# A long convolution and an MLP on one core: every transpose moved to TensorE, the cosine made from an absolute value, inverse rest columns evicted pair by pair, and a new order

## The chip, the cores and the metric

The kernel runs on one core of a Trainium2 chip. The metric is the device time of one execution in microseconds. Engines are named as in the profile: PE (TensorE), ACT (ScalarE), DVE (VectorE), POOL (GpSimd), SP (SyncE, which here only issues DMAs).

## The reference

Sequence length S = 2048, width D = 640, F = 1728, batch 1, bfloat16. Two branches share a layer norm:

```python
x = A_q
xn = _layernorm(x, axis=-1)
# branch A
k_shift = sum over t of k_pad[:, t:t + S, :] * shift_k[:, ks - 1 - t]     # ks = 4
kv = k_shift * v
y = irfft(rfft(kv padded to 2S) * rfft(ssm_k padded to 2S))[:S] + kv * ssm_D
s = xn * y
# branch B
g = silu(gelu(xn @ w1 + b1) @ w2 + b2)
return x + s * g
```

Branch A is a convolution along the sequence with a filter of length 2048 for each of the 640 columns; branch B is a two-layer MLP. (The sum is written short here; in the reference it is a loop over four shifts.)

## The kernel before

**Layout.** Rows lie as [128 partitions, 16 tiles, 640 columns]. A tile i holds one row for each partition; `x`, `xn`, `K` (the filter), `k` and `v` all have this form. The DMA work is large: 31.30 MB are read from DRAM and 18.35 MB written, the inputs and three scratch buffers of 128 x 32 rows, each written and read once. The buffer `kvl` holds k and v, and later what is loaded back from scratch.

**Branch A** is a Fourier transform in two stages, by matmuls. A table `W` [128, 16, 128] holds sines and cosines of the first stage: DVE makes the angles as whole numbers modulo 8192 (`wq`), ACT's Sin turns them into W (`ws`), in two groups (tiles 0 to 3 and 4 to 15). Stage one (`stage1`) multiplies each of the 16 tiles of K, and of the product kv, by its slice of W (`K1_i`, `U1_i` for the first 512 columns, `K1r_g`, `U1r_g` for the other 128 columns of four tiles together). The results are evicted from PSUM to the buffer `st` (`Ke`, `Ker`, `Ue`, `Uer`; st has room for four stores) and stored to `scrK` and `scrU` (`Ks_r`, `Us_r`, eight each, 640 KB). Since partitions change their meaning between the stages, the data go through DRAM: `KL_s` and `UL_s` read them back in another order. The loads can start only when all eight stores have landed.

Stage two takes 8 groups s. A small table F2 makes 32-point transforms of K and U (`K2`, `U2`, `X2` for the rest columns of both), evicted by `Kf` and `Uf`; DVE multiplies the two (`pr` for 512 columns, `qr` for the rest); the table I1 transforms back (`i1_s`, and `i1r` for the rest columns of two groups together), evicted by `ie` and `ier`; `cs_s` stores to `scrC`, `cl_r` reads back after all eight. Last come `i2_i` with the inverse table `G`, which is W with each 128x128 slice transposed, `ym_i` (DVE, times xn), `ad_i` (DVE, plus x) and the output store `os_i`.

The kv product itself is DVE work: five groups `kv0` to `kv4`, each four products with the shift weights and three sums, then times v (L524, L528, L531, L533). The weights are broadcast by `wm` and `we`.

**Branch B.** `bn`, `ep`, `rs`, `xn` are the layer norm (`ep`, `rs` on POOL mostly). The MLP's first layer needs xn transposed, `xnT`, in four chunks of four tiles. In the kernel before, tiles 0 to 7 (chunks 0 and 1) are transposed on PE (`xt`, L422, five 128x128 transposes a tile, copied out of PSUM by `xe`); chunks 2 and 3 are transposed by one DMA each (`xT2`, `xT3`, L429), and G by a third one (`gt`, L496), all from SP. `f1_c_ft_r` is the first layer (L450, `f1h` L464 for the half tile), `ge` the Gelu on ACT, `f2_i_n` the second layer for half a tile's columns (L486), `si` the Silu on ACT, `gx` the product with xn on DVE. For tiles 12 to 15 f2 comes after the convolution's end.

**Order.** Every operation is an entry of a plan, and the string `ORDER` lists all of them in the order in which they are issued. A suffix names the engine where there is a choice (`/D` DVE, `/A` ACT, `/P` POOL, `/S` SP; `/C` makes PE use two column halves), and the numbers after a colon are slots: PSUM banks (eight), quarters of st, or buffers for the loads. Each engine works through its own entries strictly in this order, so an entry that waits holds up what stands behind it on its engine. All evictions are issued in `evict` (L179 in the profile), told apart there by the tile they write: `st` is stage one, `kvl` stage two and inverse, `xnT` the transposes. `WARM` gives the number of warm-up matmuls (L699) that are put between the first entries, on zeros.

Of the kernel before, what the change touches and what calls it, by code (L numbers as in the profile page):

```python
# [112 lines left out]
def h3_block(ctx: ExitStack, tc: tile.TileContext, x_d, k_d, v_d, sk_d, K_d, D_d, w1_d, b1_d, w2_d, out_d):  # L113
# [123 lines left out]
    for g in range(2):  # L237
        a, b = TB[g], TB[g + 1]

        def wq(e, a=a, b=b):  # L240
# [4 lines left out]
            nc.vector.tensor_single_scalar(out=Pc[:, a:b, :], in_=Pc[:, a:b, :], scalar=L - 1, op=ALU.bitwise_and)
            nc.vector.tensor_single_scalar(out=Pm[:, a:b, :], in_=Pm[:, a:b, :], scalar=L - 1, op=ALU.bitwise_and)

        def ws(e, a=a, b=b):
            wv = W_t[:, a:b, :].rearrange("p t (k c) -> p t k c", c=2)
            for c, p_ in enumerate((Pc, Pm)):  # L250
                nc.scalar.activation(out=wv[:, :, :, c], in_=p_[:, a:b, :], func=ACT.Sin, scale=sc, bias=cst[:, 0:1])
# [293 lines left out]
    for s in range(NG):  # L545
# [81 lines left out]
        if z == 1:  # L627
# [12 lines left out]
            for y in range(2):  # L640

                def ier(e, y=y, pb=pb, Us=R["U"][y]):
                    q = sorted(b.slot for b in pb)
                    src = ps_t[:].rearrange("p (m n) c -> p m n c", n=2)[:, q[0] // 2:q[1] // 2 + 1:(q[1] - q[0]) // 2, :, 128 * y:128 * y + 128]
                    evict(e, Us.v[:, :, CA:D].rearrange("p (m n) c -> p m n c", n=2), src)
# [2 lines left out]
                R["C"][y].append(cw)
                op("ier_%d" % (s - 1 + y), "ACT|DVE", ier, reads=pb + R["p"][2 * y:2 * y + 2], writes=[cw], hold=[R["U"][y]])
# [57 lines left out]
ORDER = """
zz c0 grid fix xl0 id b1l skl warm9:0 warm1:1 xl3 Kl1 warm3:0 wq1 bn0 bn4 bn5 warm0:1 Kl3 warm8:0 mh bn6 Dl sm0 xl1 wm3:2 wm0:0
ep0/P warm2:4 ws1 K1_4:6.0 we0 xl2 bn7 one1 sm1 we3 K1_7:4.1 wm1:0 ep3/P rs3 Ke_7 we1 bn1 rs0 Ke_4 warm5:2 warm4:3 w1l1
K1r_3:4.2.3 xn5 Ker_6 warm6:2 K1_12:0 wm2:2 bn3 warm7:6 kl0 xn4 w1l0 xn7 w1l3 Ker_7 xn0 K1r_1:6 K1_14:4 xn6 ep1/P we2 Ke_12 w1l2  # L710
xt4:2.0 one0 xe4/D xt7:3 rs1 K1_5:0 Ke_14 Ke_5 xn1 xt6:2 xt5:4 Ker_2 xe7/D xe6/D w1l4 b1c xe5/D xt1:5.1 Ker_3 K1_6:0 K1_13:2 Ke_6
wq0 f1_1_0_0:4.1 xt0:6 xe1/D bn2 Ke_13 Kl0 K1_15:0 xe0 f1_1_9_0:5 f1_0_9_0:7.0 vl3 sm2 sm3 f1_0_2_0:6 f1_1_2_0:2 ep2/P kv0_1m:0
f1_1_8_0:3 rs2 ws0 ss Ke_15 xn3 ge_1_8_0 Ks_3/P kv0_0:1 xn2 Ks_2 xt3:0 kl1 vl0 f1_1_3_0:1 f1_1_5_0:3 xe3 kv0_1a xt2:0 ge_0_2_0
ge_1_2_0 Da ge_1_3_0 f1_1_4_0:2 ge_1_9_0 ge_1_5_0 kv0_2m:0 ge_1_4_0 f1_0_0_0:1 sx f1_0_3_0:5 xe2/D f1_0_11_0:6 f1_0_4_1:0 kv0_2a
Ks_6/P ge_0_3_0 ge_1_0_0 ge_0_11_0 ge_0_9_0 f1_0_8_1/C:3 f1_0_5_2:2 K1_0:4.2 ge_0_0_0 K1r_0:6.0 ge_0_8_1 ge_0_5_2 f1_0_4_0/C:1
f1_0_10_0/C:3 Ke_0 f1h_1:2 f1_0_1_1/C:4 kv0_3m:0 ge_0_10_0 Ker_1 ge_0_1_1 kv0_3a Ker_0/D geh_1 f1_1_10_0/C:3 f1_1_12_0/C:5 kv0_4
# [78 lines left out]
```

## Time and profile before

| | |
|---|---|
| times of three runs | 194.02, 194.5, 195.72 us; median 194.5 |
| span of the profiled execution | 191.4 us |
| its own time | not given apart from the span; the median of the runs is 3.1 us over it |
| PE busy | 175.2 us, 92% |
| DVE busy | 156.2 us, 82% |
| ACT busy | 145.4 us, 76% |
| POOL busy | 27.0 us, 14% |
| DMA | 51.82 MB, mean 271 GB/s |
| chain that ended last | PE 52%, DMA 22%, DVE 11%, ACT 8% |

Three engines are full at the same time. A busy share is an average over stages, though: up to about 40 us the DMA engines are full with inputs (over 400 GB/s for most of 10 to 35 us), then stage one and the MLP run beside one another, from about 88 us stage two, from about 164 us the last inverse step and the output. What an idle stretch of an engine costs is read from what ended it: the waits name the engine and line that waited, and who released it.

### The profile page before, as it was taken

Reading aid. Unit: us, or ns where it says so; the run is one execution under the profiler, and the core shown is the slowest. Engines: PE = TensorE matmul, PEld = TensorE weight load, DVE = VectorE, ACT = ScalarE, POOL = GpSimd, SP = SyncE. Lnnn points to the kernel's source line nnn. Section 1 sums busy time; section 2 is a strip of 40 time slices with the busy share of each in tenths; the row PEclk is TensorE's granted clock in tenths of the full one; section 3 lists DMA queues with packets and bytes.
Section 4 is the critical chain, followed back from the end, with each engine's and each line's share of the span. In section 5 each row is a group of like instructions: output and inputs, shape, how many; then the busy total and the mean of one; then the engine's idle time right before and its main releaser. Section 6 shows DMA issues by size and latency. Waiting matters only on the chain.

```text
span 191.4 us, 5365 instructions
## 1 busy us (share of the span) xinstructions
PE 175.2 (92%) x2262; PEld 104.8 (55%) x2262; DVE 156.2 (82%) x261; ACT 145.4 (76%) x227; POOL 27.0 (14%) x58
## 2 busy tenths in 40 slices
PE   7799996899999978996969999999999999989990
PEld 2235564685676545564535444444555569668780
DVE  7989797699998999799996876967999630669992
ACT  4789994999999949965866997979889867832110
POOL 4196820000100000123200100030000113000000
PEclk9969999999999999999999999999999999999998
DMA  6999999954999986769996179599712376991384
GB/s 189 375 421 419 409 423 422 424 205 155 351 358 395 335 312 276 310 241 315 364 233 191 30 252 205 170 384 339 120 39 102 140 274 206 420 415 62 102 290 160
DMA packets 26683, 51.82 MB, mean 271 GB/s; under 512 B 9122, under 2 KB 19747, under 8 KB 26276
## 3 DMA queue, kind: packets, MB, share of 16 engines
q1 hardware_dynamic: 23200, 40.06, 60.5%
q0 software_dynamic: 2304, 10.49, 14.4%
q10 hardware_dynamic: 1156, 0.95, 1.5%
q8 instruction: 17, 0.28, 0.6%
q14 instruction: 6, 0.05, 0.1%
HBM read 31.30 MB, written 18.35 MB: 259 GB/s over the span
## 4 chain that ended last, share of the span: by engine, by line
PE 52%; DMA 22%; DVE 11%; ACT 8%; POOL 2%; issue 1%; SPq 1%; ACTq 0%; DVEq 0%
PE ps L450 21%; PE ps L486 15%; DMA kvl<-scrU 7%; DMA kvl<-scrC 5%; DMA scrK<-st 4%; ACT st L179 4%; PE ps L603 4%; PE ps L358 3%; DMA x<-in_ssm_k 3%; PE ps L560 2%; DMA scrU<-st 2%; DVE xn L672 2%; DVE x L676 2%; PE ps L699 2%; ACT kvl L179 2%
## 5 line engine op out<-in xcount | busy, mean ns | idle before, releaser
L486 PE MATMUL ps<-w,hT 128*64 128x320 bf16 (+4 forms) x644 | 65.8, 294 | 0.0
L450 PE MATMUL ps<-xnT,w 128*64 128x512 bf16 (+5 forms) x550 | 62.3, 324 | 2.8 <-ACT st L179 2.4
L486 PEld LDWEIGHTS <-hT 128*64 128x64 bf16 (+3 forms) x644 | 45.6, 105 | 19.2 <-issue 6.4
L179 ACT CAST kvl<-ps 128x1024 bf16<-128x1024 f32 (+2 forms) x52 | 42.1, 847 | 10.7 <-PE ps L574 4.5
L450 PEld LDWEIGHTS <-w 128*64 128x64 bf16 (+1 forms) x550 | 33.9, 106 | 25.6 <-issue 9.2
L179 ACT CAST st<-ps 128x1024 bf16<-128x1024 f32 (+1 forms) x44 | 37.4, 958 | 6.1 <-DMA scrK<-st 2.5
L454 ACT ACTIVATE hT<-ps,b1f 128x512 bf16<-128x512 f32 (+2 forms) x71 | 36.8, 619 | 3.7 <-PE ps L450 3.3
L179 DVE CAST kvl<-ps 128x1024 bf16<-128x1024 f32 (+1 forms) x24 | 25.9, 1089 | 11.0 <-ACT kvl L179 5.2
L490 ACT ACTIVATE sl<-ps 128x320 bf16<-128x320 f32 (+1 forms) x33 | 14.1, 447 | 14.6 <-PE ps L486 8.2
L593 DVE TENSOR_TENSOR st<-kvl 128x2048 bf16<-128x2048 bf16 x16 | 19.2, 1219 | 0.4 <-ACT kvl L179 0.4
L528 DVE TENSOR_TENSOR kvl<-kvl 128x2560 bf16<-128x2560 bf16 (+1 forms) x15 | 18.3, 1221 | 0.8 <-DMA kvl<-in_k 0.6
L531 DVE TENSOR_TENSOR kvl<-kvl 128x2560 bf16<-128x2560 bf16 (+1 forms) x15 | 18.3, 1223 | 0.4
L492 DVE TENSOR_TENSOR xn<-xn,sl 128x320 bf16<-128x320 bf16 (+1 forms) x33 | 9.9, 310 | 9.9 <-ACT sl L490 9.9
L672 DVE TENSOR_TENSOR xn<-ps,xn 128x640 bf16<-128x640 f32 x16 | 12.7, 820 | 2.1 <-PE ps L668 2.0
L392 DVE BATCH_NORM_STATS2 stats<-x 128x6 f32<-128x320 bf16 x32 | 13.8, 474 | 0.1
L560 PE MATMUL ps<-kvl,F 64*32 64x512 bf16 x256 | 10.4, 380 | 1.4 <-ACT st L179 1.4
L699 PE MATMUL ps<-hT 128*128 128x512 bf16 x20 | 8.5, 577 | 1.2 <-DVE hT L223 1.2
L490 ACT ACT_TABLE_LOAD x5 | 6.4, 1283 | 3.6 <-PE ps L486 3.6
L603 PE MATMUL ps<-st,I 32*64 32x512 bf16 x256 | 8.7, 379 | 0.0
L412 DVE TENSOR_SCALAR xn<-x,mv,rstd 128x640 bf16<-128x640 bf16 x16 | 6.8, 452 | 0.9 <-POOL rstd L408 0.9
L358 PEld LDWEIGHTS <-W 64*128 64x128 bf16 x64 | 3.2, 94 | 7.4 <-issue 6.3
L652 POOL DMA_DIRECT2D scrC<-kvl x4 | 3.0, 754 | 27.6 <-ACT kvl L179 24.7
(83 smaller groups left out, 141.0 us busy)
## 6 DMA issues: line engine op xcount, KB each, us to landing
scrU<-st SPq DMA_DIRECT2D x6, 640.0 KB, 4.1
kvl<-scrK SPq DMA_DIRECT2D x6, 640.0 KB, 8.3
kvl<-scrU SPq DMA_DIRECT2D x6, 640.0 KB, 5.2
scrK<-st SPq DMA_DIRECT2D x5, 640.0 KB, 7.8
kvl<-scrC SPq DMA_DIRECT2D x5, 640.0 KB, 10.7
kvl<-in_v SPq DMA_DIRECT2D x4, 640.0 KB, 13.5
scrC<-kvl SPq DMA_DIRECT2D x4, 640.0 KB, 4.5
scrC<-kvl POOLq DMA_DIRECT2D x4, 640.0 KB, 4.5
```

What stands on the lines that cost most here:

```text
L179: (nc.scalar.copy if e == "ACT" else nc.vector.tensor_copy)(out=out_, in_=in_)
L392: nc.vector.bn_stats(out=stats[:, i, h, :], in_=x_t[:, i, h * H:(h + 1) * H])
L450: nc.tensor.matmul(out=pb.v[us, 0:n], lhsT=w1_t[:, ft, t, us], rhs=xnTb[c].v[:, a:b, t, :], start=(t == 0), stop=(t == DT - 1))
L454: nc.scalar.activation(out=hTb[c].v[:, ft, a * P:b * P], in_=pb.v[:, 0:(b - a) * P], func=ACT.Gelu_apprx_tanh, bias=b1_f[:, ft:ft + 1], sc ...
L486: nc.tensor.matmul(out=pb.v[w * u:w * u + w, 0:b - a], lhsT=hTb[c].v[0:M, ft, q * P + w * u:q * P + w * u + w], rhs=w2_t[0:M, ft, a:b], st ...
L490: op("si_%d_%d" % (i, n), "ACT", lambda e, pb=pb, s_=s_, a=a, b=b: nc.scalar.activation(out=s_.v[:, 0:b - a], in_=pb.v[:, 0:b - a], func=A ...
L528: op("kv%d_%dm" % (r, j), "DVE", lambda e, i=i, n=n, j=j, t=t, wb=wb: nc.vector.tensor_tensor(out=t.v[:, 0:n, :], in0=k_t[:, i + 3 - j:i + ...
L531: op("kv%d_%da" % (r, j), "DVE", lambda e, n=n, t=t, a=a: nc.vector.tensor_tensor(out=a.v[:, 0:n, :], in0=a.v[:, 0:n, :], in1=t.v[:, 0:n, ...
L560: nc.tensor.matmul(out=pb.v[32 * j:32 * j + 32, a, :], lhsT=F2_t[64 * a:64 * a + 64, ri, :], rhs=B.v[64 * a:64 * a + 64, j, 0:CA], start=T ...
L593: nc.vector.tensor_tensor(out=pr.v.rearrange("p (a r c) -> p a r c", a=2, r=2), in0=u, in1=k, op=ALU.mult)
L603: nc.tensor.matmul(out=pb[j // 2].v[64 * a:64 * a + 64, j % 2, :], lhsT=I1_t[32 * j:32 * j + 32, m, :], rhs=o[32 * j:32 * j + 32, a, r, :] ...
L672: op("ym_%d" % i, "DVE", lambda e, i=i, pb=pb: nc.vector.tensor_tensor(out=xn_t[:, i, :], in0=pb.v.rearrange("p a b -> p (a b)")[:, 0:D], ...
```

## The change

- **Transposes.** `DMAT = ()` and `GDMA = False`: all 16 tiles of xn go over PE (`xt`, 40 transposes more) and are copied out by ACT or DVE (`xe`, eight more), and G is made by 16 transposes on PE (`gt0`, `gt1`) and two copies (`gc0`, `gc1`, both on DVE). The three DMA transposes are gone from SP.
- **Cosine.** Before, DVE made a second angle for the cosine (an addition and a bit mask). Now ACT takes the absolute value of the angle that the sine uses, and the Sin of that, shifted by a quarter turn: two DVE operations fewer and one ACT operation more for each of the two groups.
- **Inverse rest.** `i1r` handles the rest columns of two groups y at once, spread over two pairs of banks. Before, one `ier` evicted group y from both pairs in one instruction (128x512). Now one `ier` evicts one pair of banks m for both groups, in two instructions of 128x256, and both must be done before either group is stored.
- **Warm-up.** `WARM` goes from ten entries of 2 to (3, 1, 2).
- **Order.** `ORDER` is another string throughout, with other slots and other choices of engine.

```diff
-DMAT = (2, 3)
-GDMA = True
+DMAT = ()
+GDMA = False
...
-    cst = sb.tile([P, 1], F32, name="cst")
+    cst = sb.tile([P, 2], F32, name="cst")
...
-    Pq = w2f[:, 0:4096].bitcast(I32)
-    Pm, Pc = (Pq[:, i * 1024:(i + 1) * 1024].rearrange("p (a b) -> p a b", a=NT) for i in range(2))
+    Pm, Pa = (w2f[:, i * 2048:(i + 1) * 2048].bitcast(t).rearrange("p (a b) -> p a b", a=NT) for i, t in enumerate((I32, F32)))
...
         nc.vector.memset(cst[:, 0:1], -math.pi * (1.0 - SIN_EPS))
+        nc.vector.memset(cst[:, 1:2], -math.pi / 2 * (1.0 - SIN_EPS))
...
-            nc.vector.tensor_single_scalar(out=Pc[:, a:b, :], in_=Pm[:, a:b, :], scalar=3 * L // 4, op=ALU.add)
-            nc.vector.tensor_single_scalar(out=Pc[:, a:b, :], in_=Pc[:, a:b, :], scalar=L - 1, op=ALU.bitwise_and)
...
-            for c, p_ in enumerate((Pc, Pm)):
-                nc.scalar.activation(out=wv[:, :, :, c], in_=p_[:, a:b, :], func=ACT.Sin, scale=sc, bias=cst[:, 0:1])
+            nc.scalar.activation(out=wv[:, :, :, 1], in_=Pm[:, a:b, :], func=ACT.Sin, scale=sc, bias=cst[:, 0:1])
+            nc.scalar.activation(out=Pa[:, a:b, :], in_=Pm[:, a:b, :], func=ACT.Abs, scale=sc, bias=cst[:, 0:1])
+            nc.scalar.activation(out=wv[:, :, :, 0], in_=Pa[:, a:b, :], func=ACT.Sin, scale=1.0, bias=cst[:, 1:2])
...
-            for y in range(2):
-
-                def ier(e, y=y, pb=pb, Us=R["U"][y]):
-                    q = sorted(b.slot for b in pb)
-                    src = ps_t[:].rearrange("p (m n) c -> p m n c", n=2)[:, q[0] // 2:q[1] // 2 + 1:(q[1] - q[0]) // 2, :, 128 * y:128 * y + 128]
-                    evict(e, Us.v[:, :, CA:D].rearrange("p (m n) c -> p m n c", n=2), src)
+            for m in range(2):
+
+                def ier(e, m=m, pb=pb, U=tuple(R["U"])):
+                    q = sorted(pb, key=lambda b: b.slot)
+                    for y in range(2):
+                        o = U[y].v
+                        evict(e, o[:, 2 * m:2 * m + 2, CA:D], q[m].v[:, :, 128 * y:128 * y + 128])
...
-WARM = (2,) * 10
+WARM = (3, 1, 2)
 ORDER = """
...
-kv4_1a kv4_2m:0 Uer_2 kv4_2a f2_7_0:3.1 KL3:4 Ue_7 kv4_3m:0 kv4_3a K2_0_1:0 kv4_4 Us_2/P K2_0_0:4 Ue_6 si_7_0 si_2_0 Kf_0_1
...
+kv4_3m:1 kv4_3a kv4_4 U1_4:2 K2_0_1:4 Ue_4 K2_0_0:6 Kf_0_1 Kf_0_0 f2_7_1:1.0 si_7_1 si_1_1 U1r_1:2.2 Uer_2 U1_12:4.3 U1_6:6 Ue_6
```

Line numbers of the kernel after are mostly one less than before up to the inverse rest, and one more behind it.

Three places of the new order, each engine's queue before and after. First SP, where the stores to scrU end and stage two's loads begin; L547 and L548 (L546 and L547 after) are the loads of K and U from scratch, L378 (L377) the stores. Before:

```order
L378 DMA scrU<-st 128x2560 x4
L548 DMA kvl<-scrU 128x4x640 x2
L547 DMA kvl<-scrK 128x4x640
L548 DMA kvl<-scrU 128x4x640
L429 DMA_TRANSPOSE xnT_73<-xn 128x20x128
L548 DMA kvl<-scrU 128x4x640 x2
L429 DMA_TRANSPOSE xnT_72<-xn 128x20x128
L652 DMA scrC<-kvl 128x4x640
```

After:

```order
L377 DMA scrU<-st 128x2560 x4
L546 DMA kvl<-scrK 128x4x640
L547 DMA kvl<-scrU 128x4x640 x3
L546 DMA kvl<-scrK 128x4x640
L547 DMA kvl<-scrU 128x4x640 x2
L546 DMA kvl<-scrK 128x4x640
L653 DMA scrC<-kvl 128x4x640 x4
```

One load of K now stands ahead of the first three of U, and no transpose stands between loads. Second DVE, in the last two groups of kv (L528 and L531 are product and sum, L533 the product with v, L524 the first product of a group). Before:

```order
L533 TENSOR_TENSOR kvl<-kvl 128x1280
L524 TENSOR_TENSOR kvl<-kvl 128x1280
L179 CAST st<-ps 128x2x2x128
L528 TENSOR_TENSOR kvl<-kvl 128x1280
L531 TENSOR_TENSOR kvl<-kvl 128x1280
```

After:

```order
L532 TENSOR_TENSOR kvl<-kvl 128x1280
L523 TENSOR_TENSOR kvl<-kvl 128x1280
L527 TENSOR_TENSOR kvl<-kvl 128x1280
L530 TENSOR_TENSOR kvl<-kvl 128x1280
L527 TENSOR_TENSOR kvl<-kvl 128x1280
```

The eviction of U's rest columns into st (`Uer_3`) has left DVE's queue here and stands in ACT's. Third POOL, at its first stores to scrK (L406 and L408 are `ep` and `rs` of the layer norm, L301 the scaling of the table I1). Before:

```order
L406 TENSOR_SCALAR rstd<-mv 128x2
L408 TENSOR_TENSOR rstd<-rstd,mhalf 128x2
L378 DMA scrK<-st 128x2560
L301 TENSOR_SCALAR I_83<-I_83 128x192
L378 DMA scrK<-st 128x2560 x2
L378 DMA scrU<-st 128x2560 x2
```

After:

```order
L405 TENSOR_SCALAR rstd<-mv 128x4
L407 TENSOR_TENSOR rstd<-rstd,mhalf 128x4
L377 DMA scrK<-st 128x2560 x6
L377 DMA scrU<-st 128x2560
L546 DMA kvl<-scrK 128x4x640 x2
```

Six of the eight K stores are POOL's now, where three were, and the scaling of I1 has moved behind them.

More of the change, by code (lines that the diff above doesn't have):

```diff
@@ L639, in h3_block @@
             op("i1r_%d" % (s // 2), "PE", i1r, reads=R["p"] + [R["b"], Ib], writes=pb)
[L640 to L645 removed]
+            for m in range(2):
[4 more added lines that the diff above has]
+                        evict(e, o[:, 2 * m:2 * m + 2, CA:D], q[m].v[:, :, 128 * y:128 * y + 128])
                 cw = Buf()
[L648 to L649 removed]
+                for y in range(2):
+                    R["C"][y].append(cw)
+                op("ier_%d" % (s - 1 + m), "ACT|DVE", ier, reads=pb + R["p"], writes=[cw], hold=R["U"])
             for y in range(2):
@@ L712 @@
[L712 to L715, printed above, removed]
```

91 lines of the change are left out of this document (48 added, 43 removed).

## The prediction

> **What bounds the kernel now.** I read the head of the page first, then a table of the engines' busy time by stage, then the waits and the chain of work that ended last.
>
> ```profile
> span 191.4 us, 5365 instructions
> PE 175.2 (92%) x2262; PEld 104.8 (55%) x2262; DVE 156.2 (82%) x261; ACT 145.4 (76%) x227; POOL 27.0 (14%) x58
> ...
> 0.00:17.10 17.10, 14.45 (x83) 5.42 (x83) 14.89 (x46) 12.30 (x16) 9.61 (x35) 0.90 0.90 343
> 17.10:35.00 17.90, 15.54 (x155) 9.80 (x155) 14.13 (x21) 15.41 (x29) 5.75 (x7) 1.00 1.02 419
> 35.00:80.40 45.40, 43.50 (x450) 27.99 (x447) 42.98 (x47) 42.84 (x75) 1.59 (x3) 1.00 0.82 306
> 80.40:101.00 20.60, 17.72 (x283) 10.76 (x281) 19.36 (x44) 14.17 (x23) 3.91 (x5) 1.00 0.97 294
> 101.00:152.50 51.50, 50.97 (x840) 25.02 (x838) 41.18 (x57) 44.26 (x62) 3.80 (x5) 1.00 0.61 180
> 152.50:168.30 15.80, 14.35 (x166) 10.77 (x166) 5.70 (x10) 11.62 (x16) 2.36 (x4) 1.00 0.80 294
> 168.30:187.00 18.70, 18.70 (x300) 15.04 (x300) 17.04 (x40) 4.41 (x9) 0.00 (x0) 1.00 0.57 210
> 187.00:191.40 4.40, 0.00 (x0) 0.00 (x0) 0.92 (x4) 0.44 (x1) 0.00 (x0) 0.84 0.43 149
> ```
>
> A row gives a stretch and its length, then busy time and count of PE, of its weight load, of DVE, ACT and POOL, the granted clock, the DMA share and GB/s. PE is busy 175.2 of 191.4 us. From 101 to 152.5 it idles 0.53 us, from 168.3 to 187 not at all; after its last matmul 4.4 us go by until the last output has landed. So a microsecond more on PE costs one, nearly anywhere after 17 us, and what an order can win is PE's idle time. That idle time has names:
>
> ```profile
> PE ps L574 <- DMA kvl<-scrU: 2.9, 2, 1.4
> PE ps L450 <- ACT st L179: 2.4, 1, 2.4
> PE ps L560 <- ACT st L179: 1.4, 2, 0.9
> PE ps L358 <- DMA x<-in_ssm_k: 1.2, 1, 1.2
> ...
> PE ps L668 <- DMA kvl<-scrC: 1.0, 1, 1.0
> PE ps L358 <- ACT st L179: 0.7, 2, 0.5
> ...
> ACT st L179 <- DMA scrK<-st: 2.5, 1, 2.5
> ACT st L179 <- DVE st L179: 2.4, 1, 2.4
> ...
> 24.37 8.56 DMA scrK<-st
> ...
> 69.79 0.61 DVE st L179
> ...
> 80.41 4.48 DMA scrU<-st
> ...
> 86.61 13.08 DMA kvl<-scrU
> ```
>
> The waits give us in total, times, and the longest; the chain gives start and length. Four of them have a cause in the order. (a) 2.4 us near 32: ACT's eviction waits until a store to scrK has freed its quarter of st; the store is issued at 24.37 and takes 8.56, and PE waits for ACT. (b) 1.9 us near 71 (1.4 and the longest 0.5 of the last PE row): ACT waits for a DVE cast into st, which ran only at 69.79, behind the kv products. (c) 2.9 us between 88 and 100: stage two waits twice for U coming back from scrU; the second load took 13.08. (d) 1.0 us near 168: a load from scrC.
>
> **The change part by part.**
>
> ```profile
> L179 ACT CAST kvl<-ps 128x1024 bf16<-128x1024 f32 x30 | 29.9, 1020 | 4.0 <-PE ps L603 1.9 <-PE ps L560 1.5 <-ACT hT L454 0.3
> ...
> L179 ACT CAST kvl<-ps 128x512 bf16<-128x512 f32 x18 | 10.3, 593 | 5.6 <-PE ps L574 4.5 <-PE ps L636 1.2
> ...
> L699 PE MATMUL ps<-hT 128*128 128x512 bf16 x20 | 8.5, 577 | 1.2 <-DVE hT L223 1.2
> ...
> L422 PE MATMUL ps<-ident,xn 128*128 128x128 bf16 x40 | 3.2, 219 | 0.1
> ...
> L179 DVE COPY xnT<-ps 128x640 bf16<-128x640 bf16 x6 | 2.8, 477 | 0.7 <-PE ps L422 0.7
> ...
> L251 ACT ACTIVATE W<-w,cst 128x768 bf16<-128x768 int32 x2 | 2.1, 1134 | 0.5 <-DVE w L245 0.5
> ...
> L179 ACT COPY xnT<-ps 128x640 bf16<-128x640 bf16 x2 | 1.5, 734 | 0.0
> ...
> L251 ACT ACTIVATE W<-w,cst 128x256 bf16<-128x256 int32 x2 | 1.1, 654 | 0.0
> ```
>
> *Tiles 8 to 15 on TensorE.* Forty transposes took 3.2 us of PE, 80 ns each in a stream; the change adds forty more, for tiles whose place lies after 80 us, where PE has no room: +3.2 us, all of it on the path. Their eight copies out of PSUM, seven on DVE at 0.477 and one on ACT at 0.734, lie beside PE's work; DVE had 1.2 us free between 80.4 and 101 and gets three of them there, so they have little cover, and without it would cost 1.4.
>
> *The inverse table on TensorE.* Sixteen transposes at 80 ns are 1.3 us, early: before 17.1 us PE has 14.45 us busy, and 8.5 of that is the warm-up of L699, whose 20 matmuls become 6. I take 0.6 of the 1.3 (bounds 0 and 1.3). The two copies of 128x1024 have no row of their own; between 0.477 for 640 elements and 1.020 for an eviction of 1024 I take 0.7, on DVE, behind nothing that PE waits for.
>
> *The DMA transposes go.*
>
> ```profile
> 90.02 9.87 SPq L429 DMA_TRANSPOSE xnT<-xn  x1
> 99.94 0.58 SPq L548 DMA_DIRECT2D kvl<-scrU  x1
> ...
> kvl<-scrU SPq DMA_DIRECT2D x1, 640.0 KB, 4.8
> xnT<-xn SPq DMA_TRANSPOSE x1, 11.9
> ```
>
> In this stretch SP needs 9.87 us to issue one transpose, the U load queued behind it starts at 99.94, and the transposed 640 KB land after 11.9 us where a plain load of the same size took 4.8. The load that took 13.08 us ran beside it. So without the transposes the second wait of (c), 1.4 us, goes. The Trainium skill, "Advanced Engine Details and Errata", section X-Bar Transpose (TRN2), speaks against this part: transposing DMAs are as fast as plain ones. The rows here disagree, 11.9 against 4.8. By the rule 1.4 us of the sum would stay. The first wait of (c) goes as well if the last U store comes no later: between the last U matmul and the first one that needs UL there stood four half tiles of f2, and now five and twenty transposes, whose 1.6 us alone are longer than that wait. So −2.9 for (c).
>
> *The order.* The DVE queue has no cast into st between the kv products any more, so (b) goes: −1.9. For (a), the first K stores now leave POOL's queue behind one another, without the scaling of I1 between them, and the eviction that reuses their st quarter comes after more of ACT's Gelu work; the stores themselves still run beside the input loads. Bounds 0 and −2.4; I take −2.4, since the rows of that store are now the first of all that ACT evicts. For (d) I take half, −0.5: more of f1 and f2 is left for the time in which scrC makes its round trip. The tail of 4.4 us stays.
>
> *The cosine.* It takes two DVE passes over each table group away and adds an Abs on ACT: 0.65 and 1.13 us by the rows of L251, 1.8 in sum, ahead of the first K evictions. *The pairwise inverse rest* turns eight evictions of 512 elements into sixteen of 256. From 1.020 for 1024 and 0.593 for 512 an eviction has about 0.17 fixed, so a pair of 256 is 0.76: +0.17 times eight, 1.4 us. From 101 to 152.5 ACT has 7 us free and DVE 10, so this costs nothing unless ACT becomes the bound there, and then 1.4.
>
> *What ACT gets.* Counting ACT's queue up to its last eviction of U:
>
> ```profile
> L490 ACT ACTIVATE sl<-ps 128x320 bf16<-128x320 f32 x31 | 13.6, 457 | 13.8 <-PE ps L486 7.4 <-DMA out<-x 3.5 <-DVE x L676 1.5
> ...
> L179 ACT CAST st<-ps 128x512 bf16<-128x512 f32 x13 | 7.6, 667 | 2.5 <-DVE st L179 2.4
> ...
> L179 ACT CAST kvl<-ps 128x640 bf16<-128x640 f32 x4 | 2.7, 695 | 1.0 <-PE ps L336 1.0
> ```
>
> three more rest evictions (moved from DVE, 0.667 each: 2.0), the Abs (1.8), one more copy of xnT (0.7), less one broadcast of the shift weights (0.7) and one Silu (0.46): +3.4 us. Before, ACT was busy 12.30 + 15.41 + 42.84 = 70.6 of the 80.4 us; now it needs 74.0, and an equal finish leaves it 6.4 us of idle time where it had 9.9. Of those 9.9 the 4.9 of (a) and (b) go, so it can be held, with 1.4 us to spare. That is thin, and I let a third of the 3.4 come back as new waits of PE: +1.1 (bounds 0 and 3.4). The activation tables are loaded seven times in place of eleven; the four that go all belong to the second half, where ACT is not the bound: 0.
>
> **Sum.** 3.2 + 0.6 − 2.4 − 1.9 − 2.9 − 0.5 + 1.1 = −2.8 us. The span of the profiled execution is 191.4; its own time is not given apart from that. The median of the runs is 194.5, so some 3.1 us lie around the span and stay. Forecast: span 188.6, time 191.7, 1.4% less. With the bounds the forecast's own case reaches from 189.5 (194.5 + 3.2 − 2.4 − 1.9 − 2.9 − 1.0: the table hidden, no new wait, all of (d)) to 195.2 (194.5 + 3.2 + 1.3 − 2.4 − 1.9 − 2.9 + 3.4).
>
> **Rivals.**
>
> *ACT becomes the bound up to the last U store.* Mechanism: ACT's 3.4 us come on top of an idle time that stays 9.9, because (a) only moves: the stores are still slow beside the loads, and every eviction of the first stage except one now stands in ACT's queue. Then the last U store comes at 83.8 in place of 80.4 and everything behind it shifts: +3.4, and 3.2 for the transposes behind it, less 2.9 for (c) and 0.5 for (d): 194.5 + 3.2 = 197.7, slower. For it: 42.84 busy of 45.4 us from 35 to 80.4. Against it: the 4.9 us that ACT spent in (a) and (b). It decides once ACT idles more than 6.4 us before the last U store; at 9.9 it gives the whole price. Chance 0.19.
>
> *The other waits come back, only (c) goes.* PE is as full as before and the new order meets as many late stores and casts as the old one did: 194.5 + 3.2 + 0.6 − 2.9 = 195.4, no change that can be told. Chance 0.13.
>
> *The clock.*
>
> ```profile
> 8.00:10.00 2.00, 1.98 (x9) 0.64 (x9) 1.81 (x10) 1.33 (x2) 0.33 (x2) 0.76 1.03 404
> 10.00:12.00 2.00, 2.00 (x12) 0.47 (x10) 1.92 (x6) 1.85 (x4) 1.94 (x4) 0.50 1.04 435
> 12.00:14.00 2.00, 2.00 (x17) 0.61 (x16) 1.88 (x6) 1.30 (x3) 1.85 (x5) 0.88 1.01 410
> ```
>
> Even with 20 warm-up matmuls the granted clock fell to 0.50 at 10 to 12 us, after PE had waited 1.2 us for the first K rows. With 6 there is less work before 16 us, and the fall can come later and lie over the first f1 pieces. A fall of this depth and length there costs 2 × (0.24 + 0.50 + 0.12) = 1.7 us: 193.4. Against it: at that time PE waits for ACT and for loads anyway. Chance 0.06. The Trainium skill, "TensorE: Matmul & The Clock Gate", Part 1, says that an idle window of some 3.4 us brings half clock and a busy one the full clock again. The fall here agrees in depth, but no wait of that length stands ahead of it. By that rule the loss would be half of one window, the same 1.7.
>
> *The transposes by DMA were not what slowed the U load*: its 13.08 us came from the other loads beside it. Then 1.4 stays: 193.1. Chance 0.05.
>
> **How the numbers follow.** The forecast's case has 0.57; a measurement of this kernel can tell about 1%, 1.9 us, from no change, and 0.42 of the 0.57 lies below 192.55, 0.15 above. Faster: 0.42. Within 1%: 0.15 + 0.13 + 0.06 + 0.05 = 0.39. Slower: 0.19. The range 189.3 to 197.7 leaves out about 0.05 below the first case's bound, which an earlier start of f1 could reach, and the upper half of the ACT rival, about 0.1.
>
> **What would show it.** In the profile after: PE busy near 175.2 + 4.5 − 6.0 (14 of the 20 warm-up matmuls), so about 173.7; the x transposes at 80 and about 6.4 us; no DMA transpose on SP; no PE wait of over 1 us for an eviction into st or for scrU; the last store to scrU issued by 80 us or sooner; ACT idle at most 7 us before it. If that store comes at 83 or later, the ACT rival holds. If the granted clock is below 1.00 after 16 us, the clock's does. If scrU loads still take over 10 us with nothing transposing, the transposes were not their cause. The forecast is wrong if PE shows new waits of 4 us or more in sum between 17 and 187 us.

## The result, and the profile after

The changed kernel takes 191.64 us, median of 18 runs (190.17 to 193.95); the kernel before takes 194.5 in the 18 runs beside them. The ratio is 0.9882, with a 95% interval from 0.9845 to 0.9920: 1.2% faster, 2.3 us with 1.6 to 3.0. (Some executions of a kernel take about 1% longer than the rest; no ratio counts them, but the traces of the first and the third experiment below come from such executions, each 2.3 us over the median of the runs that count.) The forecast was 191.7. So the time was right; not all of its terms were, and the runs below show which.

The profiled execution of the changed kernel has a span of 189.6 us and a time of 191.38. In the runs of the changed kernel 1.7 to 2.1 us lie between span and time, in those of the kernel before 1.7 to 1.8, not the 3.1 that the prediction worked out from a span and a median. The profiled execution of before, with its span of 191.4, was thus some 1.3 us quicker than its median, and the two traces differ by only 1.8 us.

The head of the page, and the busy time by stage (PE, weight load, DVE, ACT, POOL, then granted clock, DMA share, GB/s). The stages are cut at the same events as before: the first f1, the last store to scrU (now 77.0), the last inverse product (now 147.4), the wait for scrC (now 167.0), PE's last matmul (now 185.4).

```profile
span 189.6 us, 5651 instructions
...
PE 177.2 (93%) x2393; PEld 108.3 (57%) x2393; DVE 155.1 (82%) x263; ACT 145.5 (77%) x237; POOL 28.3 (15%) x64
```

```profile
0.00:17.10 17.10, 12.01 (x65) 5.79 (x66) 13.60 (x44) 14.82 (x20) 10.03 (x36) 1.00 0.89 333
17.10:35.00 17.90, 17.90 (x231) 12.92 (x230) 16.39 (x23) 16.27 (x34) 3.65 (x6) 1.00 1.02 416
35.00:77.00 42.00, 41.78 (x478) 26.02 (x476) 40.80 (x45) 41.80 (x70) 4.43 (x7) 1.00 0.93 352
77.00:101.00 24.00, 23.43 (x336) 14.40 (x332) 19.43 (x46) 17.44 (x27) 4.11 (x6) 1.00 0.69 235
101.00:147.40 46.40, 46.17 (x794) 22.86 (x794) 42.23 (x60) 39.39 (x63) 3.76 (x5) 1.00 0.47 155
147.40:167.00 19.60, 17.53 (x209) 11.32 (x208) 5.66 (x12) 12.27 (x18) 2.36 (x4) 1.00 0.81 306
```

PE now idles 0.2 us between 17 and 77, where it idled 4.3 between 17 and 80. From 35 to 77 us PE, ACT and DVE are all three busy for 97% or more. Behind the last store to scrU there is little idle time but one wait, and that one has grown. PE's waits after 17 us, and three pieces of the chain:

```profile
PE ps L669 <- DMA kvl<-scrC: 2.1, 1, 2.1
...
PE ps L559 <- DMA kvl<-scrU: 0.6, 1, 0.6
PE ps L357 <- ACT st L178: 0.3, 1, 0.3
PE ps L602 <- ACT kvl L178: 0.2, 1, 0.2
```

```profile
76.95 5.95 DMA scrU<-st
83.05 5.10 DMA kvl<-scrU
...
155.39 11.51 DMA kvl<-scrC
```

Of the four waits the prediction wanted gone, (a) near 32 us and (b) near 71 are gone, (c) for scrU has fallen from 2.9 to 0.6, and (d) for scrC has doubled from 1.0 to 2.1. By stage the traces compare so: the last store to scrU leaves at 76.95, before at 80.41, 3.5 us earlier; from there to the end of the last inverse product it takes 70.4 us, before 72.1, 1.6 less although 40 transposes were added; from there to the end 42.2, before 38.9, 3.3 more. In sum −1.8.

The new work on PE, and the first products of f1 with the same products later, as groups and as the timeline has them (start, length):

```profile
L421 PE MATMUL ps<-ident,xn 128*128 128x128 bf16 x80 | 7.1, 236 | 1.3 <-DVE xn L411 1.1
...
L504 PE MATMUL ps<-ident,W 128*128 128x128 bf16 x16 | 1.7, 265 | 0.0
```

```profile
16.79 1.27 PE L449 MATMUL ps<-xnT,w 128*128 128x256 bf16 x5
...
24.43 0.71 PE L449 MATMUL ps<-xnT,w 128*128 128x256 bf16 x5
```

The transposes take 7.1 us in place of 6.4, and PE as a whole 177.2 in place of the 173.7 forecast. The second fence shows the larger part of why: the same five products of 128x256 take 1.27 us at 16.8 and 0.71 at 24.4. Until 19.7 us all matmuls run at about half their later speed, though the granted clock in the stage table reads 1.00.

### The profile page after: what moved, and what is told of

Its sections match the earlier page's. It is cut to its first block, busy times and chain, and to the rows that moved or that the text cites. A ratio compares the mean times of both kernels' runs of the same rounds, so it can differ in the third digit from the quotient of the medians.

```text
span 189.6 us, 5651 instructions
## 1 busy us (share of the span) xinstructions
PE 177.2 (93%) x2393; PEld 108.3 (57%) x2393; DVE 155.1 (82%) x263; ACT 145.5 (77%) x237; POOL 28.3 (15%) x64
## 4 chain that ended last, share of the span: by engine, by line
PE 59%; ACT 17%; DMA 17%; DVE 2%; issue 2%; SPq 0%
PE ps L485 24%; PE ps L449 18%; ACT st L178 9%; DMA kvl<-scrC 6%; ACT hT L453 5%; DMA b1r<-in_b 4%; PE ps L559 4%; PE ps L602 4%; DMA scrU<-st 3%; DMA kvl<-scrU 3%; PE ps L357 2%; PE ps L421 2%; PE ps L669 2%; DMA x<-in_x 2%; PE ps L635 1%
## 5 line engine op out<-in xcount | busy, mean ns | idle before, releaser
L485 PE MATMUL ps<-w,hT 128*64 128x320 bf16 (+3 forms) x728 | 65.7, 295 | 0.0
L449 PE MATMUL ps<-xnT,w 128*64 128x512 bf16 (+5 forms) x555 | 63.1, 324 | 0.0
L485 PEld LDWEIGHTS <-hT 128*64 128x64 bf16 (+2 forms) x728 | 46.9, 107 | 17.5 <-issue 5.5
L178 ACT CAST kvl<-ps 128x1024 bf16<-128x1024 f32 (+3 forms) x59 | 43.5, 796 | 8.2 <-PE ps L559 3.4
L449 PEld LDWEIGHTS <-w 128*64 128x64 bf16 (+1 forms) x555 | 33.3, 107 | 24.4 <-issue 6.2
L178 ACT CAST st<-ps 128x1024 bf16<-128x1024 f32 (+1 forms) x47 | 39.1, 935 | 1.9 <-PE ps L357 1.8
L489 ACT ACTIVATE sl<-ps 128x320 bf16<-128x320 f32 (+1 forms) x33 | 14.2, 448 | 22.5 <-PE ps L485 22.0
L178 DVE CAST kvl<-ps 128x1024 bf16<-128x1024 f32 (+3 forms) x25 | 23.7, 968 | 3.5 <-ACT kvl L178 1.5
L421 PE MATMUL ps<-ident,xn 128*128 128x128 bf16 x80 | 7.1, 236 | 1.3 <-DVE xn L411 1.1
L669 PE MATMUL ps<-kvl,G 128*64 128x512 bf16 (+1 forms) x64 | 5.7, 299 | 2.1 <-DMA kvl<-scrC 2.1
L421 PEld LDWEIGHTS <-xn 128*128 128x128 bf16 x80 | 5.7, 106 | 3.1 <-DVE xn L411 1.4
L377 POOL DMA_DIRECT2D scrK<-st x6 | 3.5, 579 | 24.3 <-ACT st L178 24.3
```

Source lines behind the costliest of these rows:

```text
L178: (nc.scalar.copy if e == "ACT" else nc.vector.tensor_copy)(out=out_, in_=in_)
L421: nc.tensor.transpose(out=o[:, t, :], in_=xn_t[:, i, t * P:(t + 1) * P], identity=ident[:])
L449: nc.tensor.matmul(out=pb.v[us, 0:n], lhsT=w1_t[:, ft, t, us], rhs=xnTb[c].v[:, a:b, t, :], start=(t == 0), stop=(t == DT - 1))
L485: nc.tensor.matmul(out=pb.v[w * u:w * u + w, 0:b - a], lhsT=hTb[c].v[0:M, ft, q * P + w * u:q * P + w * u + w], rhs=w2_t[0:M, ft, a:b], st ...
L489: op("si_%d_%d" % (i, n), "ACT", lambda e, pb=pb, s_=s_, a=a, b=b: nc.scalar.activation(out=s_.v[:, 0:b - a], in_=pb.v[:, 0:b - a], func=A ...
```

## Experiments

Twelve kernels. "Ratio" is against the kernel before, whose own runs stand beside each; the changed kernel's is 0.9882, and 1% is 1.9 us. The changed kernel did not run again beside them, so a difference between two such ratios is known to 1.1 to 1.4 us. Each keeps all of the computation; some do a piece of it twice and say so.

### The transposes of x back to DMA, in the new order

```diff
-DMAT = ()
+DMAT = (2, 3)
 (xt8..xt15, xe8..xe15 out of the order; behind UL1: xT2:1, behind xn12: xT3:0)
```

> The changed kernel, with the tiles 8 to 15 of x transposed by two DMAs again, in the new order. My theory (PE is full; the transposing DMA slows the loads of U beside it): PE is rid of 3.2 us, but a load of U takes over 10 us again and PE waits for it 1.4 us, and the first wait for U grows from 0.6 to about 1.5, since no transposes stand ahead of it: 191.6 - 3.2 + 1.4 + 0.9 = 190.7. Rival (the DMA transposes cost no one anything): 188.4. Rival (SP's queue behind the transposes holds more loads up than in the kernel before): 193 to 195.

Ratio 0.9895 (0.9834 to 0.9956): no difference from the changed kernel that these runs can tell. PE's waits in this trace, in total, times, longest:

```profile
PE ps L559 <- DVE st L592: 2.2, 1, 2.2
PE ps L559 <- DMA kvl<-scrU: 2.1, 1, 2.1
...
PE ps L559 <- DMA kvl<-scrK: 1.0, 1, 1.0
```

PE is rid of 3.2 us and gets 4.7 of new waits in stage two of this trace: 1.5 more for scrU near 88, where the twenty transposes stood between the last product of stage one and the first that needs U, and 2.2 + 1.0 near 130, behind the second transpose on SP. (Of the 1.5 a part may be chance: the wait for scrU near 88 is 0, 0.6 and 1.2 us in the traces of three kernels that do not differ up to there: the one of wait (d), the changed kernel, and the one with half of the transposes late.) The rival of 188.4 falls. By the times the two prices are about the same, so that this part of the change, by itself, is worth nothing in the new order, to within 1.4 us either way.

How long the transposes take to land themselves, as the group of DMA issues has it (KB left out there, median us to landing):

```profile
xnT<-xn SPq DMA_TRANSPOSE x2, 8.0
```

8.0 us, 8.6 and 7.3 apart, not 11.9 as in the kernel before. The plain loads of U from SP have a median of 7.0 in the same execution.

### Only the transposes of x on PE, in the old order

```diff
-DMAT = (2, 3)
+DMAT = ()
-Uf_3_1 xT2:1 ep5 pr_2_0:0 ...
+Uf_3_1 ep5 xt8:7.1 pr_2_0:0 ... xe8/D Uf_3_2 xt9:4 xe9/D ... xt10:5 xe10/D X2_1:2 ... xt11:7 xe11/D f2_0_0:7.0
 (tiles 12 to 15 likewise, where xT3 stood)
```

> The kernel before, in its old order, with only one part of the change made: tiles 8 to 15 of x transposed on PE, their copies on DVE, no x transpose by DMA. My theory: +3.2 us on PE, and of the two waits for U the second, 1.4 us, goes, while the first stays, since these transposes stand behind it: 194.5 + 1.8 = 196.3. Rival (the DMA transposes were not what slowed the load): the wait stays, 197.7. Rival (both waits go and the queue on SP moves up): 194.5 or less.

Ratio 1.0413 (1.0334 to 1.0492), 8 us slower, beyond every expectation. PE's waits, and the stage around 100 us:

```profile
PE ps L486 <- DVE xnT L179: 2.5, 1, 2.5
...
PE ps L574 <- DMA kvl<-scrU: 1.4, 1, 1.4
```

```profile
99.00:103.00 4.00, 2.96 (x22) 1.58 (x29) 1.65 (x4) 0.00 (x0) 0.00 (x0) 0.79 0.14 47
103.00:107.00 4.00, 4.00 (x70) 2.17 (x62) 3.14 (x4) 2.28 (x4) 0.00 (x0) 0.79 0.02 4
```

A piece of f2 needs the PSUM bank of the last transpose, whose copy stands on DVE behind the products and evictions of stage two: 2.5 us of waiting, and behind it the granted clock falls: it is 0.79 on the mean of the 8 us from 99.

Of the two waits for scrU one is left, as term (c) said. But its reason is not the prediction's. The loads of U issued on SP between 84 and 90 us, here without any transpose beside them:

```profile
kvl<-scrU SPq DMA_DIRECT2D x4, 640.0 KB, 13.1
```

The load issued at 86.63 took 13.1 us, as it did before (13.08), with nothing transposing. The next load of U, which the transpose no longer holds up on SP, goes out beside it. So it still landed near 99.7; PE only came to its product later, since it had the transposes to do and waited for their copies.

### The same with other places

Each transpose was given a bank that is free there, and two of the copies went to ACT.

```diff
-... xt9:4 xe9/D ... xt10:5 xe10/D ... xt11:7 xe11/D
+si_0_1 xt8:6.1 ... xe8/D ... K2_4_1:2 xt9:6 ... xe9 ... xt10:6 ... xe10/D X2_0:4 ... xt11:6 ... xe11/D
```

> The kernel before, in its old order, with tiles 8 to 15 of x transposed on PE once more, but each transpose put where its PSUM bank is free and ahead of no piece that needs the bank at once; in the first try PE waited 2.5 us for a copy out of PSUM on DVE near 98 and the granted clock fell behind that wait. Theory: without such a wait the part costs its 3.2 us less the second wait for U: 196.3 (ratio 1.009). Rival (in the old order DVE and ACT have no room for eight more copies between 95 and 125 us, wherever they stand): 198 to 202.

Ratio 1.0627 (1.0535 to 1.0720): worse still, the rival's side and beyond. Three rows of its stage table:

```profile
103.00:107.00 4.00, 3.22 (x14) 1.81 (x13) 2.69 (x5) 0.00 (x0) 0.00 (x0) 0.64 0.02 4
131.00:134.00 3.00, 0.41 (x8) 0.22 (x8) 3.00 (x4) 0.83 (x1) 0.00 (x0) 1.00 0.31 37
134.00:138.00 4.00, 3.76 (x20) 1.83 (x19) 1.92 (x3) 1.34 (x3) 1.50 (x2) 0.61 1.05 369
```

From 131 to 134 PE is busy 0.41 of 3.0 us, while DVE is busy all of it; after that the granted clock is 0.61 over 4 us. PE's waits are short ones, 0.2 to 1.8 us, some ten of them, for copies of xnT and for evictions that now stand behind them. The bare 3.2 us of the transposes are the smaller part of their price in an order that has no room for their copies. In the changed kernel's order these copies make no wait of PE over 0.2 us.

### More warm-up

```diff
-WARM = (3, 1, 2)
+WARM = (3, 1, 3, 2, 1, 2)
-... wm3:6 we3 warm2:2 K1_13 ... K1_4:4.2 K1r_1:0.3 Ker_2
+... warm3:6 wm3:6 we3 warm2:2 K1_13 ... warm4:4 K1_4:4.2 K1r_1:0.3 warm5:2 Ker_2
```

> The changed kernel with 6 more warm-up matmuls (12 in place of 6), put into gaps in which PE waits, before 14 us. In the changed kernel the matmuls run at about half their later speed until 19.7 us (a K1 pair 0.61 in place of 0.39), in the kernel before until 13.6. Theory (PE's clock follows how full it was): the step to full speed comes at 14 to 16 us, PE needs up to 2.0 us less between 15.4 and 19.7, and about 1.2 of it come through: 190.4. Rival (the slow matmuls come from loads beside them, not from what went ahead): no step earlier, 191.6 to 192.1. Rival (PE is early anyway and waits for ACT and DVE instead): step earlier, 191.6.

Ratio 0.9886 (0.9830 to 0.9942): nothing gained. PE's timeline at the first f1, and the chain:

```profile
16.43 0.71 PE L449 MATMUL ps<-xnT,w 128*128 128x256 bf16 x5
```

```profile
20.38 0.75 POOL scrK L377
21.13 11.37 DMA scrK<-st
32.57 0.58 ACT st L178
```

The first f1 runs at full speed here, at 16.4 us, so the half speed until 19.7 in the changed kernel goes with how little PE had done before, and not with the loads beside it. PE is 1.4 us further on at 20 us. And nothing comes of it: ACT waits until 32.57 for a store to scrK, PE then waits for ACT, and the last store to scrU leaves no earlier than in the changed kernel.

### The old cosine

```diff
+ tensor_single_scalar(out=Pc, in_=Pm, scalar=3 * L // 4, op=add); ... bitwise_and
- activation(W[..., 1], Pm, Sin); activation(Pa, Pm, Abs); activation(W[..., 0], Pa, Sin)
+ activation(W[..., 0], Pc, Sin); activation(W[..., 1], Pm, Sin)
```

> The changed kernel with the old cosine: two more DVE passes over each table group (about 1.7 us on DVE), no Abs on ACT (1.4 us less by the rows of after). Theory (ACT is close behind PE up to 55 us, so part of what it gets ahead of the first K evictions counts): 191.2, last store to scrU 0.3 to 0.8 us earlier. Rival (ACT sets the end of stage one): 190.2. Rival (DVE's normalisation of x is what the first f1 waits for, and comes later by the two passes): 192 to 193.

Ratio 0.9883 (0.9826 to 0.9941): the same. The last store to scrU, in the chain:

```profile
77.05 5.70 DMA scrU<-st
```

It is 0.1 us from where it was. ACT's 1.4 us for the Abs, and the two DVE passes in their place here, come before 10 us, and neither moves that store.

### Wait (a) alone: POOL's scaling behind the store, in the kernel before

```diff
-... f1_0_0_0:1 sx f1_0_3_0:5 ... Ks_6/P ge_0_3_0
+... f1_0_0_0:1 f1_0_3_0:5 ... Ks_6/P sx ge_0_3_0
```

> The kernel before with one step of POOL moved: the scaling of I1 (1.6 us at 22.8) behind the store to scrK that stood behind it. Theory of the prediction's term (a), where a wait of PE that goes is time gained: the store is issued at 22.8 in place of 24.37, PE's wait for the st quarter near 32 falls from 2.4 to about 0.9, time 194.5 - 1.5 = 193.0. Rival (in 28 to 75 us PE, ACT and DVE are all full, and the input loads keep the DMA engines full until 50, so the store lands when it does): the wait stays at 2 us or more, or comes back within the stage, last store to scrU at 80 or later, time 194 to 194.6.

Ratio 1.0021 (0.9973 to 1.0069): nothing. The store in the chain, and PE's wait:

```profile
23.53 10.74 DMA scrK<-st
```

```profile
PE ps L450 <- ACT st L179: 2.9, 1, 2.9
```

The store is issued 0.8 us sooner and lands at 34.3, 1.3 later than before. In this stretch the DMA engines are full with input loads (share 1.0), and the store lands when they let it. Four traces agree: issued at 21.1 (more warm-up), 23.5, 23.9 (the next experiment) and 24.4 us (the kernel before), the store that ACT waits for landed at 32.5, 34.3, 32.5 and 32.9.

### Wait (b) alone: Uer_3 on ACT, in the kernel before

```diff
-Uer_3/D
+Uer_3
```

> The kernel before with one cast into st, Uer_3, on ACT in place of DVE. Theory of the prediction's term (b): the ACT wait of 2.4 us for that cast goes, PE's waits near 71 go from 1.9 to 0, ACT pays 0.67 us for the cast: last store to scrU near 79, time 194.5 - 1.3 to 1.9 = 192.6 to 193.2. Rival (ACT is as full as PE there and the wait comes back later in the stage): last store to scrU at 80 to 80.5, time 194.0 to 194.6.

Ratio 0.9929 (0.9889 to 0.9968): 1.4 us faster, as expected. Two stores to scrU, the second of them the last one:

```profile
68.84 5.32 DMA scrU<-st
...
79.41 4.34 DMA scrU<-st
```

The last one leaves 1.0 us earlier than the 80.41 of before. ACT's wait for the cast on DVE is no longer among the waits, and PE's waits near 71 are gone. But the rival is in the trace too, in part: ACT has a new wait at 74.2, for a store to scrU that frees its quarter of st, and PE waits for ACT 0.9 and 0.5 us at 76 and 77. The store that ACT waits for is the first of the two rows, landing at 74.2.

### Wait (d): one piece of f2 ahead of the waiting product, in the changed kernel

```diff
-cl_6:10 i2_13:0 ad_5 ym_6 f2_13_0/C:6.1 ad_7 ym_1 i2_0:2
+cl_6:10 ad_5 ym_6 f2_13_0/C:6.1 i2_13:0 ad_7 ym_1 i2_0:2
```

> The changed kernel with one f2 half tile (2.07 us of PE) moved ahead of the i2 product that waits 2.07 us for its load from scrC at 166.9. Theory (term (d) failed only by the place of that product: PE had other work ready): the wait goes to 0.3 or less, nothing else waits, last matmul near 183.4, time 191.6 - 1.9 = 189.7. Rival (the next product then waits for the next load, since the eight loads take all DMA engines from 155 to 167): half of it comes back, 190.6. Rival (the tail behind the last matmul grows, since the last output tiles depend on that product): 191 to 191.6.

Ratio 0.9778 (0.9721 to 0.9836): 189.52 us in its own runs, 1.0% under the changed kernel and 2.2% under the one before. PE's timeline at the place:

```profile
163.31 0.71 PE L669 MATMUL ps<-kvl,G 128*64 128x512 bf16 x8
163.85 2.07 PE L485 MATMUL ps<-w,hT 128*64 128x320 bf16 x28
166.07 0.73 PE L669 MATMUL ps<-kvl,G 128*64 128x512 bf16 x8
```

No wait for scrC is left, and no other took its place: 0.15 us lies between the f2 piece and the product. This is the best version of the study.

### ACT and PE loaded by themselves

In the first of these four Gelu evictions of 128x512 are done twice, in the second two f1 pieces of 128x512 are computed twice, both in the changed kernel between 30 and 46 us.

```diff
+ for _ in range(2 if c == 1 and ft in (0, 2, 3, 11) else 1):
     activation(hT, ps, Gelu, ...)
```

> The changed kernel with four Gelu evictions of 128x512 between 30 and 46 us done twice: 2.4 us more on ACT, nothing more on PE or DVE. From 28 to 75 us ACT is busy 46.9 of 47.1 us, PE 46.9, DVE 45.8. Theory (ACT is a bound there, beside PE): last store to scrU 2 us later, at 79, time 191.6 + 2.4 = 194.0. Rival (ACT only fills time in which PE's results queue up, with slack): under 0.8 us, 191.6 to 192.4.

```diff
- for t in range(DT):
+ for t in [q for _ in range(2 if c == 1 and ft in (0, 2) else 1) for q in range(DT)]:
```

> The changed kernel with two f1 pieces of 128x512 between 30 and 40 us computed twice: about 2.3 us more on PE, nothing more on ACT or DVE. Theory (PE is a bound in that stretch): time 191.6 + 2.3 = 193.9, and ACT waits for PE. Rival (ACT alone sets the pace until 55 us, PE is ahead of it): under 0.8 us, 191.6 to 192.4.

More on ACT: ratio 0.9956 (0.9913 to 0.9999), 1.4 us slower than the changed kernel. More on PE: 0.9882 (0.9828 to 0.9936), no slower that these runs can tell, though its trace has a span of 190.7 us against 189.6. The stretch from 28 to 56 us and SP's last stores to scrU, of the changed kernel, then with more on ACT, then with more on PE:

```profile
28.00:56.00 28.00, 27.80 (x320) 16.72 (x317) 27.59 (x21) 27.91 (x54) 1.59 (x3) 1.00 0.93 382
```

```profile
70.57 6.70 SPq L377 DMA_DIRECT2D scrU<-st  x4
```

```profile
28.00:56.00 28.00, 25.78 (x280) 14.99 (x276) 27.56 (x22) 27.81 (x50) 1.59 (x3) 1.00 0.92 358
```

```profile
73.07 6.70 SPq L377 DMA_DIRECT2D scrU<-st  x4
```

```profile
28.00:56.00 28.00, 28.00 (x311) 16.52 (x309) 27.59 (x21) 26.80 (x49) 1.59 (x3) 1.00 0.95 375
```

```profile
72.10 6.70 SPq L377 DMA_DIRECT2D scrU<-st  x4
```

With 2.4 us more on ACT the stores leave 2.5 later, and PE, which had looked full, has 2 us to spare. With 2.3 more on PE they leave 1.5 later and ACT gets room. So ACT is the bound of the two, and PE is behind it by less than a microsecond (2.3 − 1.5 = 0.8, one trace each). DVE, busy 27.59 of the 28 us in all three, was not loaded by itself, so whether it binds as well stays open. And not all of a delay at 77 us reaches the end: the waits for scrU and scrC, 0.6 and 2.1 us, take some of it up (with more on PE they are 0 and 1.4).

### Half of the transposes back to DMA, late

On top of the moved product: tiles 12 to 15 by DMA, issued at 116.8 us.

```diff
-DMAT = ()
+DMAT = (3,)
 (xt12..xt15, xe12..xe15 out of the order; behind xn12: xT3:0)
```

> The changed kernel with the i2 product moved as in the run before, and tiles 12 to 15 of x transposed by DMA (tiles 8 to 11 stay on PE), the transpose issued near 117 us, where no load is waited for. Theory (a DMA transpose costs only what waits for the loads beside or behind it, a PE transpose its 80 ns): PE is rid of 20 transposes, 1.6 us, no new wait: 189.5 - 1.6 = 187.9. Rival (what PE is rid of comes back as a wait for ACT or DVE in 101 to 147, or the transpose holds up a store to scrC): 189.5.

Ratio 0.9983 (0.9908 to 1.0057): 2% slower than the same kernel without it, though PE has 20 transposes less to do. PE's waits, SP's queue, and the stretch that follows the wait:

```profile
PE ps L559 <- DMA kvl<-scrU: 3.7, 2, 2.5
```

```profile
116.78 3.68 SPq L428 DMA_TRANSPOSE xnT<-xn  x1
120.57 0.51 SPq L547 DMA_DIRECT2D kvl<-scrU  x1
```

```profile
126.00:132.00 6.00, 3.72 (x42) 1.01 (x42) 1.71 (x2) 2.91 (x4) 0.00 (x0) 0.72 0.63 231
```

In the changed kernel PE waits for no load at that place. But the transpose has to wait for the normalised x, until 116.8, and the last U load on SP stands behind it. In the changed kernel that load left at 110.4, the second of this row:

```profile
86.39 24.41 SPq L547 DMA_DIRECT2D kvl<-scrU  x2
```

With the transpose it leaves at 120.57 and lands at 128.0, and PE waits 2.5 us for it, and over the next 6 us the granted clock is 0.72. That is more than the 1.6 us saved. (The other 1.2 of the 3.7 lie at 88 us, ahead of the transpose, and are not its doing.) It is the queue that cost here: the load was late because it was issued late.

### G by DMA and the old inverse rest

```diff
-GDMA = False
+GDMA = True
 (gt0, gc0, gt1, gc1 out of the order; gt behind KL6)
-for m in range(2): ier: evict(U[y], q[m]) for both y
+for y in range(2): ier: evict(U[y], all of q)
```

> The changed kernel with two small parts undone: the table G transposed by DMA again (issued near 122 us), and the inverse rest columns evicted in eight pieces of 512 again. Theory (both lie beside other work: the 16 transposes of G come ahead of the stretch in which PE, ACT and DVE are all full, and ACT has room from 101 to 147): 191.0 to 191.8. Rival (the 16 transposes, 1.7 us of PE at half speed before 20 us, all lay on the path): 190.0. Rival (the old eviction makes the first product of the pair wait): 192 to 193.

Ratio 1.0003 (0.9958 to 1.0047): 1.2% slower than the changed kernel, all of its gain. PE's timeline, the rows with waits for evictions:

```profile
109.38 0.44 PE L421 MATMUL ps<-ident,xn 128*128 128x128 bf16 x5 [0.85 <-ACT kvl L178]
110.49 2.32 PE L449 MATMUL ps<-xnT,w 128*128 128x512 bf16 x10 [0.67 <-ACT kvl L178]
...
123.57 1.24 PE L449 MATMUL ps<-xnT,w 128*128 128x512 bf16 x5 [0.71 <-ACT kvl L178]
125.59 0.44 PE L421 MATMUL ps<-ident,xn 128*128 128x128 bf16 x5 [0.78 <-DVE kvl L178]
...
149.49 1.07 PE L602 MATMUL ps<-st,I 32*64 32x512 bf16 x32 [1.02 <-ACT kvl L178]
```

These five are 4.0 us, for evictions into kvl; the changed kernel has 0.2 of that kind. Each instruction of the old eviction reads both pairs of PSUM banks, so both are held until the last one; an instruction of the new one reads one pair, and the order has pieces in the pair that comes free first. So the third expectation holds, and by more than it said. That the banks are the reason, and that it was the eviction and not G's transposition, is argued from these rows and the order; the two were undone together, and no run parts them. What G's transposes cost PE early can be told: without them SP's last store to scrU leaves within 0.3 us of where it was, so it is nothing.

## Why the prediction was right, and where it was not

**The result of the sum** was right: −2.8 against −2.3 (1.6 to 3.0), and the side and size of the change with it. It was right with errors of both signs in its terms, so that it came so near is in part luck. One premise failed as well: "a microsecond more on PE costs one, nearly anywhere after 17 us". Between 30 and 40 us of the changed kernel 2.3 us more on PE cost nothing that could be told.

**Term (b), −1.9**: right. Done alone it gave 1.4 us (0.6 to 2.2), and the prediction's mechanism, a cast behind the kv products, is the one that was taken away. Of PE's 1.9 us near 71, 1.4 came back at 76 and 77 in that trace, so the term may be somewhat too large.

**Term (a), −2.4**: the wait is gone, but of the two reasons given the first failed: "the first K stores now leave POOL's queue behind one another, without the scaling of I1 between them". With the store issued 0.8 us sooner the wait stayed (2.9). With more warm-up the changed kernel still has ACT waiting until 32.6 us for a store issued at 21.1. The second, that the eviction comes "after more of ACT's Gelu work", fits the trace: the new order gives PE and ACT f1 pieces before that time, and ACT evicts into st from 30.4 to 32.9 us without a wait for a store. No run parts this reason from the rest of the order.

**Term (c), −2.9**: 2.3 of it came in the trace, but the step "The load that took 13.08 us ran beside it. So without the transposes the second wait of (c), 1.4 us, goes" is wrong. With the transposes on PE in the old order the same load still took 13.1 us; that was the prediction's own sign that the transposes were not the cause, and the rival with 0.05 has the cause right as far as the runs go: with a plain load in the transpose's place it took as long. Six plain loads of that size are issued between 85 and 88 us in the kernel before, two of them on POOL, and then the transpose. In the changed kernel five go out from SP between 83 and 87 and none from POOL until 98.6; the one issued at 86.39 landed after 8.9 us, and the loads of U from SP have a median of 7.7:

```profile
kvl<-scrU SPq DMA_DIRECT2D x5, 640.0 KB, 7.7
```

So, it seems, the order of the loads won this (no run changes it alone), with the transposes of x on PE as cover near 88 (1.5 us, by the first run). Nor was 11.9 against 4.8 a measure of a transpose: both belong to that crowd, the one inside it, the other behind it. The Trainium skill, "Advanced Engine Details and Errata", section X-Bar Transpose (TRN2), has transposing DMAs as fast as plain ones; 8.0 against 7.0 in the first run is near it, and the prediction was wrong to set it aside. What a transpose does cost is SP: 3.2 to 9.9 us to issue one, and what stands behind it waits.

**The transposes on PE, +3.2**: as bare PE time right (3.9 for the added 40, of 7.1, some of it the half speed of the first ones). As a price it depends on the order: nothing against the DMA in the new one, 8 to 12 us in the old one. The prediction gave their copies 1.4 us at most.

**The inverse table, +0.6**: 0. It takes 1.7 us of PE, ahead of 20.3 us, and PE's time there buys nothing, as the warm-up run shows.

**Term (d), −0.5**: wrong in sign, +1.1. The failed step is "more of f1 and f2 is left for the time in which scrC makes its round trip". More was left, about 2 us of f2 by the traces (22.5 us behind the last inverse product, before 20.5), but not ahead of the product that waits: PE takes its queue in order, and the piece that could have covered the wait stood behind it. One piece moved gave all of it back, 2 us.

**ACT, +1.1, and its rival**: the loss was not there; ACT's idle time before the last U store fell from 9.9 us to 4.1, with (a) and (b), as the term argued, and the store left 3.5 us earlier. But the rival's mechanism was closer than its 0.19 says: ACT does bound the changed kernel from 28 to 56 us, and a load of 2.4 us on it passes on in full to that store. The rival's number, 197.7, was wrong since ACT's idle time did fall.

**The inverse rest pair by pair**: called free, at worst 1.4 us of ACT. It gains, probably some 2 us, through the PSUM banks (argued, see the last experiment); the prediction counted evictions and did not ask when each bank comes free.

**The clock's rival**: half speed did lie over the first f1 pieces, as it feared, and cost nothing. Its sign to look for was useless, since the granted clock reads 1.00 there. The other sign, new waits of 4 us or more, did not come: 2.1 and 0.6.

**The other waits come back**: refuted by 0.2 us of idle PE from 17 to 77 us.

Where the time went, by the traces: 3.5 us won by the last U store (2.6 forecast: (a), (b), +1.1, +0.6), 1.6 us won up to the last inverse product (0.3 lost forecast: +3.2 and (c)), 3.3 us lost behind it (0.5 won forecast). The last two hang together, since the order moved f2 from the one to the other, and the forecasts of the three stretches missed by 0.9, 1.9 and −3.8 us: in their sum most of it cancels.

## What to carry to other kernels

A wait at the head of an in-order queue is cured by what stands ahead of it, not by how much work there is: count the ready work between the last product and the waiting one. An edit that costs an engine so many microseconds costs that only where its PSUM bank and its copy out have a place; in an order made without it the same edit cost two to four times its bare time. And where three engines are full in one stretch, load each of them by itself: busy time could not tell ACT from PE here, but 2.4 us more on ACT moved the last store by 2.5 and 2.3 more on PE by 1.5.
